# A convolution stage rebuilt: 24 frequency units in two interleaved halves of the batches, unsplit fp32 inverse transforms, filter product with exchanged partition halves

## The chip, the cores and the metric

The kernel runs on one core of one Trainium2 chip. The metric is the device time of one execution in microseconds (us); lower is better. The engines are named as the profile names them: PE (TensorE), DVE (VectorE), ACT (ScalarE), POOL (GpSimd) and SP (SyncE, which here only issues transfers).

## The reference

```python
X = np.fft.rfft(x, axis=1)                    # x: 8 batches x 3072 x 256, fp32
F = (filt_r + 1j * filt_i)[None, :, :]
x = np.fft.irfft(X * F, n=3072, axis=1)       # the convolution; then 24576 tokens of 256
do = x @ w_skip > 0                           # routed part: the best of 8 experts
e = argmax(x[do] @ w_gate);  g = softmax(...)[e]
x[do] += g * (relu(x[do] @ w1[e]) @ w2[e])
h = x @ w_in                                  # 256 -> 2048, all tokens
g = (a0 + a1*h + a2*h^2 + a3*h^3) / (1 + |b0||h| + |b1|h^2 + 1e-6)
out = g @ w_out                               # 2048 -> 256
```

The change touches only the first three lines of this and the routing that is done along with them.

## The kernel before, in words

Three stages follow one another. `conv` computes the convolution and sorts the tokens by expert. `table` and `moe_phase` run the experts in 28 slots of 512 tokens. `ff` runs the last network in 48 groups. Nothing of a later stage starts before the last token is sorted.

Inside `conv` a transform of 3072 points is split as 48 x 64. It goes through memory three times:

- **A** (`step_a`, 64 steps: 4 pairs of batches x 16 slices): loads 96 partitions of `x` (48 points of each of two batches), multiplies by the constant `fwd` into 25 complex frequencies (100 rows for the two batches), evacuates by ACT and stores into the memory tensor `za`, one store for each batch.
- **B** (`step_b`, 50 units: 25 frequencies k x 2 halves c of the batches): loads 128 partitions of `za`, multiplies by `mid` twice (mm 0 gives real over imaginary part, mm 1 imaginary over real), multiplies each by a filter table on DVE (`mult`, tiles t), adds the two on POOL (`add`), multiplies by `midi`, evacuates by ACT and stores into `zv`. `tables` loads `mid`, `midi` and the filter tables for five frequencies at a time.
- **C** (`step_c`, 64 steps; `batch` after every four): loads `zv`, multiplies by `inv`, evacuates and stores the tokens into `yd`; then transposes them on PE, multiplies by the routing weights, transposes back, and for each of 16 batches of 1536 tokens counts the positions and issues 12 indirect transfers on POOL (`scatter`, `lst<-pair,di`), which write the token numbers into the list `lst`.

Every fp32 product of A, B and C is made of three products of rounded parts (`mm3`): ACT rounds the operand to a high part (`hi`, tiles sh, yh), DVE subtracts it to get a low part (`lo`, tiles sl, yl; 26 of the 50 in B are on POOL), and PE multiplies high by high, low by high and high by low.

The order of instructions is made at build time by `Plan`: every operation has an engine, a duration, a rank and the tiles that it reads and writes, and each engine takes, of what could start, the one of least rank. The rank is a step's time t plus an offset by kind (`C_RANK`). Before, t runs on from A through B to C by `C_STEP`. Each engine then runs its queue in that order. PSUM tiles are P (2 buffers) and Q (2).

B of a half needs every `za` of that half; C of a batch needs every `zv` of its half.

Of the kernel before, what the change touches and what calls it, by code (L numbers as in the profile page):

```python
# [14 lines left out]
ALU = mybir.AluOpType  # L15
# [7 lines left out]
NK1 = 25  # L23
# [43 lines left out]
ZLO_POOL = 26  # L67
C_SLACK, C_AHEAD, C_STEP = 0.2, 12.0, (1.955, 3.997, 3.209)
C_BUFS = {'ld': 9, 'sh': 4, 'sl': 3, 't1': 4, 't2': 2, 'ev': 3, 'kt': 2, 'rh': 2, 'rl': 3, 'lt': 2, 'P': 2, 'Q': 2, 'yh': 2, 'yl': 2}
C_RANK = {'a_load': -9.13, 'a_hi': -5.41, 'a_lo': 4.16, 'a_mm': -1.53, 'a_evac': 0.65, 'a_store': 2.61, 'k_load': -35.12, 'k_filt': -24.74, 'k_sign': -13.7, 'b_load': -16.35, 'b_hiz': -5.44, 'b_loz': -1.99, 'b_mm': -2.42, 'b_mult': -0.87, 'b_add': 3.77, 'b_hiy': 5.63, 'b_loy': 6.8, 'b_mmi': 7.04, 'b_evac': 6.58, 'b_store': 10.59, 'c_load': -10.78, 'c_hi': -2.7, 'c_lo': -1.61, 'c_mm': 3.14, 'c_evac': 1.03, 'c_store': -3.1, 'c_tr': 4.44, 'c_rhi': 3.82, 'c_rlo': 2.18, 'c_logit': 9.08, 'c_lt': 6.85, 'c_back': 7.94, 'c_l9': 9.04, 'r_top': 9.23, 'r_ex': 7.28, 'r_pick': 8.67, 'r_count': 11.74, 'r_gate': 16.29, 'r_place': 14.7, 'r_scatter': 16.76}  # L70
# [13 lines left out]
def _constants():  # L84
    k1 = np.arange(NK1)
    n1 = np.arange(N1)
    n2 = np.arange(N2)
    t = 2 * np.pi * ((n1[:, None] * k1[None, :]) % N1) / N1
    fwd = np.zeros((2, N1, 2, NK1, 2))
    inv = np.zeros((2, NK1, 2, 2, N1))  # L90
    wk = np.where((k1 == 0) | (k1 == N1 // 2), 1.0, 2.0) / SEQ
    for r in range(2):
        fwd[r, :, r, :, 0] = np.cos(t)
        fwd[r, :, r, :, 1] = -np.sin(t)
        inv[r, :, 0, r, :] = (np.cos(t) * wk).T
        inv[r, :, 1, r, :] = (-np.sin(t) * wk).T
    k = k1[:, None] + N1 * n2[None, :]
# [4 lines left out]
    mid = np.concatenate([re, im, re], 2)  # L102
    c, s = c.transpose(0, 2, 1), s.transpose(0, 2, 1)
    midi = np.concatenate([np.concatenate([c, s], 2), np.concatenate([-s, c], 2)], 1)
    sg = np.where((k == 0) | (k == SEQ // 2), 0.0, np.where(k > SEQ // 2, -1.0, 1.0))
    sgn = np.stack([np.concatenate([-sg[i], sg[i]]) for i in (0, 1)], 1)
# [6 lines left out]
        "fwd": _split(fwd.reshape(2 * N1, 4 * NK1)).transpose(1, 0, 2),  # L113
        "inv": _split(inv.reshape(4 * NK1, 2 * N1)).transpose(1, 0, 2),
        "mid": _split(mid).transpose(2, 1, 0, 3),
        "midi": _split(midi).transpose(2, 1, 0, 3),
# [109 lines left out]
class Net:  # L226
# [23 lines left out]
    def setup(self):  # L250
        nc, a = self.nc, self.a
        dp = self.pool(self.ctx, "dram", 1, DRAM)
        self.za = dp.tile([NK1, 2, N2, NB, D], F32, name="za")
        self.zv = dp.tile([NK1, 2, N2, NB, D], F32, name="zv")
# [42 lines left out]
    def conv(self):  # L297
# [3 lines left out]
        G = 5  # L301
# [4 lines left out]
        fwd = cp.tile([2 * N1, 2, 4 * NK1], F32R, name="fwd")  # L306
        inv = cp.tile([4 * NK1, 2, 2 * N1], F32R, name="inv")
# [8 lines left out]
        def ps(tag):  # L316
            return pp.tile(T, F32, tag=tag, name=tag, bufs=2)
# [13 lines left out]
        def consts():  # L331
            V.memset(lists["none"], 0.0)
            nc.gpsimd.dma_start(fwd, a["fwd"])

        def consts2():
            nc.gpsimd.dma_start(inv, a["inv"])
            nc.sync.dma_start(sgn, a["sgn"])
# [3 lines left out]
        p.op("POOL", 1.1, -100, consts, writes=["fwd"], lag=2.0)  # L341

        def step_a(u, s, t):
            o = {}
            ms = slice(4 * s, 4 * s + 4)
            x = a["x"][2 * u:2 * u + 2].rearrange("r (n m) d -> (r n) m d", n=N1)
            zo = za.rearrange("k i m b d -> b (k i) m d")
# [5 lines left out]
            def hi():  # L353
                o["h"] = tl("sh", F32R)[0:2 * N1]
                nc.scalar.copy(o["h"], o["x"])

            def lo():
                o["l"] = tl("sl", F32R)[0:2 * N1]
                V.tensor_tensor(out=o["l"], in0=o["x"], in1=o["h"].bitcast(F32), op=ALU.subtract)

            def mm():
                o["p"] = ps("PQ"[s % 2])[0:4 * NK1]
                for h in range(2):
                    hs = slice(2 * h, 2 * h + 2)
                    self.mm3(o["p"][:, hs], fwd[:, 0], fwd[:, 1], o["h"][:, hs], o["l"][:, hs])

            def evac():
                o["o"] = tl("ev")[0:4 * NK1]
# [6 lines left out]
            kx, kh, kl, kp, ko = [k + (n,) for n in "xhlpo"]  # L375
            p.op("SP", 1.1, t + R["a_load"], load, writes=[new(kx, "ld")], lag=2.0)
            p.op("ACT", act(1024, 1), t + R["a_hi"], hi, reads=[kx], writes=[new(kh, "sh")])
            p.op("DVE", dve(1024), t + R["a_lo"], lo, reads=[kx, kh], writes=[new(kl, "sl")])
            p.op("PE", 1.3, t + R["a_mm"], mm, reads=["fwd", kh, kl], writes=[new(kp, "PQ"[s % 2])])
            p.op("ACT", act(1024), t + R["a_evac"], evac, reads=[kp], writes=[new(ko, "ev")])  # L380
            for r in range(2):
                p.tile(("za", u, s, r), ("za", u, s, r), 1)
                p.op("SP", 0.57, t + R["a_store"], store, r, reads=[ko], writes=[("za", u, s, r)], lag=2.0)

        def tables(g, t):
            o = {}
            ks = slice(G * g, G * g + G)

            def load():
                kt[g] = mid, midi, fr, fi = [  # L390
                    sp.tile(s, dt, tag=n, name=n, bufs=bufs["kt"])
                    for n, s, dt in (("mid", [128, G, 2, 192], F32R), ("midi", [128, G, 2, 128], F32R), ("fr", [128, G, D], F32), ("fi", [128, G, D], F32))
                ]
                nc.gpsimd.dma_start(mid, a["mid"][:, ks])
                nc.gpsimd.dma_start(midi, a["midi"][:, ks])

            def filt(h):
                _, _, fr, fi = kt[g]
# [11 lines left out]
            new(("k", g), "mid", "kt")  # L410
            new(("f", g), "fil", "kt")
            p.op("POOL", 2.1, t + R["k_load"], load, writes=[("k", g)], lag=5.0)
            for h in range(2):
                p.op("SP", 2.0, t + R["k_filt"], filt, h, reads=[("k", g)], writes=[("f", g)], lag=2.0)
            p.op("DVE", 0.9, t + R["k_sign"], sign, reads=["inv"], writes=[("f", g)])

        def step_b(k, c, t):
            o = {}
            g, j = divmod(k, G)
            zi = za.rearrange("k i m (c b) d -> k c (i m) b d", c=2)  # L420
            zo = zv.rearrange("k i m (c b) d -> k c (i m) b d", c=2)
# [12 lines left out]

            def mm(w):
                m = kt[g][0]
                o[w] = ps("P")
                ws = slice(64 * w, 64 * w + 128)
                for h in range(2):
                    hs = slice(2 * h, 2 * h + 2)  # L440
                    self.mm3(o[w][:, hs], m[:, j, 0, ws], m[:, j, 1, ws], o["h"][:, hs], o["l"][:, hs])
# [9 lines left out]
            def mmi():  # L451
                m = kt[g][1]
                o["p"] = ps("Q")
                for h in range(2):
                    hs = slice(2 * h, 2 * h + 2)
                    self.mm3(o["p"][:, hs], m[:, j, 0], m[:, j, 1], o["h"][:, hs], o["l"][:, hs])
# [5 lines left out]
            def store():  # L462
                nc.sync.dma_start(zo[k, c], o["o"])

            q = ("b", k, c)
            K = {n: q + (n,) for n in ("z", "h", "l", 0, 1, "y0", "y1", "yh", "yl", "p", "o")}
            deps = [("za", u, s, r) for u in (2 * c, 2 * c + 1) for s in range(16) for r in range(2)]
# [653 lines left out]
```

## Time and profile before

| | |
|---|---|
| time, median of 3 runs (lowest, highest) | 3947.9 us (3943.36, 3948.54) |
| span of the profiled execution, first to last instruction | 3942.5 us |
| `conv`, to the start of the last scatter | 812.7 us |
| first expert matmul | 834.06 us |

The profiled execution has no time of its own in the profile beside its span. Against the lowest run 0.9 us lies around the span, against the median 5.4 us. All times below are from the span's start. [...]

### The profile page before, as it was taken

To read this page: it belongs to the slowest core of one execution; us is meant where nothing else is said; L and a number is where in the kernel's file an instruction comes from. 1 tells how busy PE (TensorE), PEld (TensorE's weight loads), DVE (VectorE), ACT (ScalarE), POOL (GpSimd) and SP (SyncE) were. 2 spreads that over 40 slices of the span, in tenths; PEclk is the share of its full clock that TensorE was granted. 3 is DMA by queue.
4 is the path that set the end of the run, shared out by engine and by line. 5 is a ranking of instruction groups with operands and counts; after the bars stand their busy time and mean duration, and the time that the engine had idled before them with its cause. 6 is when DMAs were issued, how large, how long until landed. Compare 5 with 4: busy or idle time off the path is not lost.

```text
span 3942.5 us, 54305 instructions
## 1 busy us (share of the span) xinstructions
PE 3594.7 (91%) x20164; PEld 3031.8 (77%) x20164; DVE 3106.5 (79%) x3100; ACT 3017.2 (77%) x3076; POOL 3029.8 (77%) x1661
## 2 busy tenths in 40 slices
PE   6978888749999997999999999999999999999998
PEld 3446656448888886888888888888888888888887
DVE  3369977636666664888888888888888888888887
ACT  5655577524333334999999999999999999999997
POOL 0058847743333334999999999999999999999998
PEclk6589999869999998999999999999999999999999
DMA  8877667434444441000000000000000000000000
GB/s 263 255 227 249 201 221 207 130 112 141 145 142 149 135 129 42 22 22 22 22 22 22 22 22 20 20 21 20 19 22 22 22 22 22 22 22 22 22 11 17
DMA packets 189361, 320.69 MB, mean 81 GB/s; under 512 B 27712, under 2 KB 138379, under 8 KB 189094
## 3 DMA queue, kind: packets, MB, share of 16 engines
q1 hardware_dynamic: 170374, 281.25, 22.7%
q0 software_dynamic: 18720, 35.93, 3.0%
q8 instruction: 161, 2.64, 0.3%
q14 instruction: 106, 0.87, 0.1%
HBM read 199.98 MB, written 119.25 MB: 81 GB/s over the span
## 4 chain that ended last, share of the span: by engine, by line
POOL 29%; PE 18%; issue 11%; ACT 10%; DVE 7%; DMA 3%; SPq 1%; POOLq 0%; DVEq 0%; ACTq 0%
POOL w L990 14%; POOL gl L1034 6%; POOL v L987 5%; PE psh L246 3%; PE psh L248 3%; PE psh L247 3%; POOL es L1021 3%; PE psa L855 3%; PE psa L857 3%; DVE t L993 3%; PE psa L856 3%; DMA wr<-in_moe_w_dram 2%; ACT u L978 2%; ACT lq L1000 1%; DVE t L997 1%
## 5 line engine op out<-in xcount | busy, mean ns | idle before, releaser
L990 POOL TENSOR_TENSOR w<-v,ha 128x1024 f32<-128x1024 f32 x384 | 923.4, 2405 | 16.4 <-DVE psr L1011 0.4
L246 PE MATMUL psh<-xh,wih 128*128 128x512 f32 x1536 | 614.8, 400 | 63.2 <-DVE t L997 59.8
L993 DVE TENSOR_TENSOR t<-u,psh 128x1024 f32<-128x1024 f32 x384 | 467.0, 1216 | 236.5 <-ACT ha L981 132.0
L248 PE MATMUL psh<-xh,wil 128*128 128x512 f32 x1536 | 606.9, 395 | 0.0
L247 PE MATMUL psh<-xl,wih 128*128 128x512 f32 x1536 | 604.6, 394 | 1.6 <-POOL xl L961 1.6
L1034 POOL TENSOR_TENSOR gl<-g,gh 128x1024 fp32r<-128x1024 f32 x240 | 578.2, 2409 | 5.0 <-ACT gh L1031 5.0
L857 PE MATMUL psa<-woh,gl 128*128 128x256 f32 x1920 | 537.6, 280 | 47.8 <-POOL gl L1034 47.8
L855 PE MATMUL psa<-woh,gh 128*128 128x256 f32 x1920 | 537.8, 280 | 0.0
L856 PE MATMUL psa<-wol,gh 128*128 128x256 f32 x1920 | 532.6, 277 | 0.0
L1043 PE MATMUL psa<-woh,gn 128*128 128x256 f32 x2304 | 520.5, 379 | 0.0
L997 DVE SCALAR_TENSOR_TENSOR t<-t,co,psh 128x1024 f32<-128x1024 f32 x384 | 490.0, 1276 | 5.1
L1043 PEld LDWEIGHTS psa<-woh,gn 128*128 128x128 f32 x2304 | 436.8, 190 | 64.3
L1000 ACT ACTIVATE lq<-w,cb 128x1024 f32<-128x1024 f32 x384 | 442.9, 1153 | 44.4 <-POOL w L990 44.2
L978 ACT ACTIVATE u<-psh,co 128x1024 f32<-128x1024 f32 x384 | 460.9, 1200 | 13.2 <-PE psh L248 9.4
L804 POOL DMA_INDIRECT yd<-yo,lt x112 | 131.2, 1171 | 402.2 <-DVE yo L801 376.6
L1004 ACT ACTIVATE psr<-lq 128x1024 f32<-128x1024 f32 x384 | 393.5, 1025 | 58.9 <-DVE gn L1028 57.7
L987 POOL TENSOR_SCALAR v<-ha,co 128x1024 f32<-128x1024 f32 x336 | 406.7, 1210 | 11.9 <-ACT ha L981 11.9
L857 PEld LDWEIGHTS psa<-woh,gl 128*128 128x128 f32 x1920 | 361.4, 188 | 58.1 <-POOL gl L1034 58.0
L246 PEld LDWEIGHTS psh<-xh,wih 128*128 128x128 f32 x1536 | 290.1, 189 | 134.2 <-issue 77.5
L981 ACT ACTIVATE ha<-psh 128x1024 f32<-128x1024 f32 x384 | 389.5, 1014 | 2.8 <-PE psh L248 2.8
L856 PEld LDWEIGHTS psa<-wol,gh 128*128 128x128 f32 x1920 | 361.1, 188 | 8.2
L1021 POOL TENSOR_TENSOR es<-qq,rs 128x1024 f32<-128x1024 f32 x144 | 345.0, 2396 | 29.0 <-ACT qq L1018 29.0
(181 smaller groups left out, 9063.7 us busy)
## 6 DMA issues: line engine op xcount, KB each, us to landing
wr<-in_moe_w_dram SPq DMA_DIRECT2D x224, 256.0 KB
za<-ev SPq DMA_DIRECT2D x128, 200.0 KB
ld<-za SPq DMA_DIRECT2D x50, 512.0 KB
zv<-ev SPq DMA_DIRECT2D x50, 512.0 KB
ld<-zv SPq DMA_DIRECT2D x128, 200.0 KB
ld<-in_x_dram SPq DMA_DIRECT2D x64, 384.0 KB
yd<-ev SPq DMA_DIRECT2D x64, 384.0 KB
x<-yd SPq DMA_DIRECT2D x48, 512.0 KB
```

The lines of the kernel that those rows point to most:

```text
L246: mm(out, wh, xh, start=start, stop=False)
L247: mm(out, wh, xl, start=False, stop=False)
L248: mm(out, wl, xh, start=False, stop=stop)
L855: mm(out, xh, wh, start=start, stop=False)
L856: mm(out, xh, wl, start=False, stop=False)
L857: mm(out, xl, wh, start=False, stop=stop)
L978: nc.scalar.activation(out=tl(i, "u"), in_=o["h", i], func=AF.Identity, scale=a[3], bias=a[2])
L987: nc.gpsimd.tensor_scalar(out=tl(i, "v"), in0=o[i, "ha"], scalar1=b[1], scalar2=b[0], op0=ALU.mult, op1=ALU.add)
L990: nc.gpsimd.tensor_tensor(out=tl(i, "w"), in0=o.pop((i, "v")), in1=o.pop((i, "ha")), op=ALU.mult)
L993: V.tensor_tensor(out=tl(i, "t2", 3), in0=o.pop((i, "u")), in1=o["h", i], op=ALU.mult)
L1034: nc.gpsimd.tensor_tensor(out=tl(i, "gl", 2, F32R), in0=o.pop((i, "g")), in1=o[i, "gh"].bitcast(F32), op=ALU.subtract)
L1043: nc.tensor.matmul(o["a"][:, c], x[:, f, 128 * c:128 * c + 128], self.woh[i][:, f], start=i == 0 and f == 0 and c % 2 == 0, stop=i == 7 an ...
```

## The change

The 25 frequencies of the first factor become 24 units. Frequency 24 is real in its transform, and so is frequency 0; they share unit 0, whose tables hold both (`_bins` gives the filter rows). A's tile has 96 rows and needs one store, and C's needs one load.

`za` and `zv` become two tensors each, one for each half of the batches, laid out with the batch outermost. A row of A's store is then 4 KB that lie together, and a row of B's transfers is four pieces of 1 KB (before it was the other way round).

A's product, B's second product and C's product take fp32 operands directly (`native`, two matmuls of 512 columns), without `hi` and `lo`. B's first product keeps the three-part form and is done once instead of twice: for the second filter product DVE reads the upper 64 partitions of the PSUM tile and writes the lower 64, and then the other way round.

The order: A of the first half, then A of the second half among B of the first, then B of the second half among C of the first, then C of the second half, with new ranks and durations. `tables` runs for each half, four frequencies at a time. `fwd`, `inv` and `midi` go through SP's queue instead of POOL's. PSUM tiles are P (3 buffers) and a small S (2).

```diff
-NK1 = 25
+NK = 24
-ZLO_POOL = 26
-C_SLACK, C_AHEAD, C_STEP = 0.2, 12.0, (1.955, 3.997, 3.209)
+ZLO_POOL = (0, 1, 2, 6, 8, 12, 14, 16, 19, 28, 29, 35, 42, 43)
+C_SLACK, C_AHEAD = 0.188, 18.19
+C_PACE = ((1.831, None, None), (4.868, 6.169, None), (None, 8.8, 6.593), (None, None, 5.384))
+C_START = (0.0, 62.39, 71.2, 224.0, 227.63, 440.01)
...
-        self.za = dp.tile([NK1, 2, N2, NB, D], F32, name="za")
+        self.za = [dp.tile([NB // 2, NK, 2, N2, D], F32, name=f"za{c}") for c in range(2)]
...
-            return pp.tile(T, F32, tag=tag, name=tag, bufs=2)
+            return pp.tile(T if tag == "P" else [128, 512], F32, tag=tag, name=tag, bufs=bufs[tag])
...
+        def native(out, w, x):
+            for h in range(2):
+                hs = slice(2 * h, 2 * h + 2)
+                nc.tensor.matmul(out[:, hs], w, x[:, hs], start=True, stop=True)
...
             def mm():
-                o["p"] = ps("PQ"[s % 2])[0:4 * NK1]
-                for h in range(2):
-                    hs = slice(2 * h, 2 * h + 2)
-                    self.mm3(o["p"][:, hs], fwd[:, 0], fwd[:, 1], o["h"][:, hs], o["l"][:, hs])
+                o["p"] = ps("P")[0:4 * NK]
+                native(o["p"], fwd, o["x"])
...
-            def store(r):
-                nc.sync.dma_start(zo[2 * u + r][:, ms], o["o"][2 * NK1 * r:2 * NK1 * (r + 1)])
+            def store():
+                nc.sync.dma_start(zo[:, ms], o["o"])
...
-                    for n, s, dt in (("mid", [128, G, 2, 192], F32R), ("midi", [128, G, 2, 128], F32R), ("fr", [128, G, D], F32), ("fi", [128, G, D], F32))
+                    for n, s, dt in (("mid", [128, G, 2, 128], F32R), ("midi", [128, G, 128], F32), ("fr", [128, G, D], F32), ("fi", [128, G, D], F32))
...
             def mult(w):
-                o["y", w] = tl(f"t{w + 1}")
-                V.tensor_tensor(out=o["y", w], in0=o[w], in1=kt[g][2 + w][:, j].unsqueeze(1).to_broadcast(T), op=ALU.mult)
+                o["y", w] = y = tl(f"t{w + 1}")
+                f = kt[c, g][2 + w][:, j].unsqueeze(1)
+                if w == 0:
+                    V.tensor_tensor(out=y, in0=o["x"], in1=f.to_broadcast(T), op=ALU.mult)
+                    return
+                for h in range(2):
+                    ss = slice(64 - 64 * h, 128 - 64 * h)
+                    V.tensor_tensor(out=y[64 * h:64 * h + 64], in0=o["x"][ss], in1=f[ss].to_broadcast([64, 4, D]), op=ALU.mult)
...
             def mmi():
-                m = kt[g][1]
-                o["p"] = ps("Q")
-                for h in range(2):
-                    hs = slice(2 * h, 2 * h + 2)
-                    self.mm3(o["p"][:, hs], m[:, j, 0], m[:, j, 1], o["h"][:, hs], o["l"][:, hs])
+                o["p"] = ps("P")
+                native(o["p"], kt[c, g][1][:, j], o["y"])
...
+        t = C_START
+        for u in range(4):
+            run_a(u, t[0 if u < 2 else 1] + u % 2 * 16 * C_PACE[u >= 2][0])
+        for c in range(2):
+            run_b(c, t[2 + c])
+        for b in range(16):
+            pace = C_PACE[2 + b // 8][2]
+            run_c(b, t[4 + b // 8] + b % 8 * 4 * pace, pace)
```

On POOL's queue, where B ends and the sorting is done, before (L449 is `add`, L433 `lo`, L628 `scatter`):

```order
L449 TENSOR_TENSOR t_3101<-t_3101,t_3157 128x1024
L449 TENSOR_TENSOR t_3166<-t_3166,t_3183 128x1024
L628 DMA lst<-pair,di 201216x2 x192
L830 TENSOR_LOAD over
```

and the same place of the change (L467 is `add`, L446 `lo`, L626 `scatter`):

```order
L467 TENSOR_TENSOR t_3142<-t_3142,t_3162 128x1024
L626 DMA lst<-pair,di 201216x2 x3
L467 TENSOR_TENSOR t_3279<-t_3279,t_3298 128x1024
L626 DMA lst<-pair,di 201216x2 x7
L467 TENSOR_TENSOR t_3334<-t_3334,t_3339 128x1024
L626 DMA lst<-pair,di 201216x2 x2
L467 TENSOR_TENSOR t_3429<-t_3429,t_3439 128x1024
L626 DMA lst<-pair,di 201216x2 x120
L833 TENSOR_LOAD over
```

Of the 192 scatters 72 now stand among the additions of B's second half, and 120 behind the last one.

On SP's queue, where A ends and B begins, before (L351 loads x, L372 stores za, L425 loads za, L463 stores zv):

```order
L351 DMA ld<-in_x_dram 96x1024
L372 DMA za<-ev 50x4x256 x2
L425 DMA ld<-za 128x1024
L372 DMA za<-ev 50x4x256 x6
L425 DMA ld<-za 128x1024
L372 DMA za<-ev 50x4x256 x6
L425 DMA ld<-za 128x1024 x5
L463 DMA zv<-ev 128x1024
```

and of the change where B of the first half begins (L379 loads x, L390 stores za, L438 loads za, L478 stores zv; za_60 is the first half's, za_61 the second's):

```order
L390 DMA za_60<-ev 96x1024 x3
L379 DMA ld<-in_x_dram 96x1024
L390 DMA za_60<-ev 96x1024
L412 DMA midi<-in_midi_dram 128x512
L413 DMA fr<-in_filt_r_dram 128x1024
L414 DMA fi<-in_filt_i_dram 128x1024
L438 DMA ld<-za_60 128x4x256 x2
L379 DMA ld<-in_x_dram 96x1024
L438 DMA ld<-za_60 128x4x256
L390 DMA za_61<-ev 96x1024
L379 DMA ld<-in_x_dram 96x1024
```

Loads and stores of A's second half now stand between those of B's first half; a store of A is one transfer of 96 rows instead of two of 50.

## Rows read from the trace of the kernel before

**Rows 1.** The page: span, and 40 equal slices of it in busy tenths.
```profile
span 3942.5 us, 54305 instructions
...
POOL 0058847743333334999999999999999999999998
...
DMA  8877667434444441000000000000000000000000
```

**Rows 2.** Windows by stage: A, B, C; busy us of PE, PEld, DVE, ACT, POOL; PEclk, DMA share, GB/s.
```profile
0.00:225.00 225.00, 175.76 (x394) 95.53 (x395) 82.66 (x77) 130.68 (x130) 4.27 (x11) 0.58 0.85 258
225.00:515.00 290.00, 232.07 (x892) 172.75 (x890) 260.06 (x176) 148.57 (x150) 237.28 (x82) 0.94 0.67 216
515.00:775.00 260.00, 229.70 (x1555) 155.31 (x1556) 200.06 (x502) 200.79 (x273) 175.14 (x162) 0.91 0.71 200
```

**Rows 3.** Windows of 25 us: within A, within B, and B's last one.
```profile
100.00:125.00 25.00, 23.66 (x52) 12.95 (x51) 10.07 (x9) 16.54 (x17) 0.00 (x0) 0.50 0.84 274
350.00:375.00 25.00, 22.19 (x93) 16.71 (x92) 23.55 (x17) 14.51 (x15) 24.98 (x11) 1.00 0.99 310
...
475.00:500.00 25.00, 22.11 (x92) 16.70 (x93) 25.00 (x20) 12.29 (x13) 24.58 (x8) 1.00 0.26 105
```

**Rows 4.** DMA issues: count and KB of each.
```profile
za<-ev SPq DMA_DIRECT2D x128, 200.0 KB
ld<-za SPq DMA_DIRECT2D x50, 512.0 KB
...
ld<-in_x_dram SPq DMA_DIRECT2D x64, 384.0 KB
...
lst<-fill SPq DMA_DIRECT2D x12, 131.0 KB
```

**Rows 5.** Timeline of PE in A, at the lower clock: start, us.
```profile
99.87 0.63 PE L246 MATMUL Q<-sh,fwd 96*100 96x512 f32 x1
...
100.29 0.63 PE L247 MATMUL Q<-sl,fwd 96*100 96x512 f32 x1
```

**Rows 6.** Timeline of PE at the full clock: B (two rows), then `ff`'s unsplit product.
```profile
250.66 0.40 PE L247 MATMUL P<-sl,mid 128*128 128x512 f32 x1
...
250.89 0.40 PE L248 MATMUL P<-sh,mid 128*128 128x512 f32 x1
...
2001.90 3.62 PE L1043 MATMUL psa<-woh,gn 128*128 128x256 f32 x16
```

**Rows 7.** Timeline of PE in C: from a back-transpose (L546) to the second routing product after it.
```profile
567.58 0.35 PE L546 MATMUL Q<-eye,lt 18*128 18x18 f32 x3
...
569.19 0.57 PE L535 MATMUL P<-rh,w9a 128*18 128x384 f32 x2
```

**Rows 8.** Lines of DVE in B (225 to 515): busy us, mean ns, idle before.
```profile
L433 DVE TENSOR_TENSOR yl<-t,yh 128x1024 fp32r<-128x1024 f32 x49 | 97.4, 1990 | 11.4 <-ACT yh L429 11.3
L445 DVE TENSOR_TENSOR t<-P,fi 128x1024 f32<-128x1024 f32 x48 | 58.1, 1212 | 3.9 <-PE P L248 3.6
L433 DVE TENSOR_TENSOR sl<-ld,sh 128x1024 fp32r<-128x1024 f32 x22 | 40.5, 1846 | 0.0
```

**Rows 9.** Lines of POOL and DVE in A, B and C.
```profile
L449 POOL TENSOR_TENSOR t<-t,t 128x1024 f32<-128x1024 f32 x50 | 154.5, 3096 | 262.4 <-DVE t L445 259.4 <-PE Q L248 1.6
...
L359 DVE TENSOR_TENSOR sl<-ld,sh 96x1024 fp32r<-96x1024 f32 x64 | 78.1, 1220 | 131.9 <-ACT sh L355 129.8 <-PE Q L247 2.1
L503 DVE TENSOR_TENSOR sl<-ld,sh 100x1024 fp32r<-100x1024 f32 x64 | 77.2, 1222 | 11.0 <-ACT sh L499 10.7 <-DMA ld<-zv 0.3
```

**Rows 10.** Timeline of POOL: first scatter, last two scatters.
```profile
549.96 1.88 POOL L628 DMA_INDIRECT lst<-pair,di  x1 [40.95 <-DVE di L625]
...
811.42 0.98 POOL L628 DMA_INDIRECT lst<-pair,di  x1 [0.30 <-issue]
812.71 0.98 POOL L628 DMA_INDIRECT lst<-pair,di  x1 [0.30 <-issue]
```

**Rows 11.** Waits from 520 to 830: engine, line <- cause: us, times, longest.
```profile
POOL lst L628 <- issue: 53.9, 177, 0.3
```

More of the change, by code (lines that the diff above doesn't have):

```diff
@@ L101, in _constants @@
     im = np.concatenate([-s, c], 1)
[L102 to L106, printed above, removed]
+    ct, st = c.transpose(0, 2, 1), s.transpose(0, 2, 1)
+    midi = np.concatenate([np.concatenate([ct, st], 2), np.concatenate([-st, ct], 2)], 1)
+    k = _bins()[0]
+    t = 2 * np.pi * ((n2[:, None] * k[None, :64]) % SEQ) / SEQ
+    c, s = np.cos(t), np.sin(t)
+    s[:, 0] = -((-1.0) ** n2)
+    lo = np.arange(64) < 32
+    re[0] = np.concatenate([c * lo, c * ~lo])
+    im[0] = np.concatenate([-s * lo, -s * ~lo])
+    w = np.where(np.arange(64) == 0, 1.0, 2.0)
+    midi[0] = np.concatenate([re[0] * w, im[0] * w], 1).T
+    mid = np.concatenate([re, im], 2)
+    sg = np.where(n2 >= 32, -1.0, 1.0)
+    one = np.where(n2 == 0, 0.0, 1.0)
+    sgn = np.stack([np.concatenate([x, -x]) for x in (one, sg)], 1)
     p = np.arange(128)
@@ L470, in step_b @@
-            pool = (2 * k + c) * ZLO_POOL // 50 != (2 * k + c + 1) * ZLO_POOL // 50
-            p.op("POOL" if pool else "DVE", 2.31 if pool else dve(1024), t + R["b_loz"], lo, "z", "sl", nc.gpsimd if pool else V, reads=[K["z"], K["h"]], writes=[new(K["l"], "sl")])
-            for w in range(2):
-                p.op("PE", 1.3, t + R["b_mm"] + w, mm, w, reads=[("k", g), K["h"], K["l"]], writes=[new(K[w], "P")])
-            for w in range(2):
-                p.op("DVE", dve(1024), t + R["b_mult"] + w, mult, w, reads=[K[w], ("f", g)], writes=[new(K[f"y{w}"], f"t{w + 1}")])
@@ L476, in step_b @@
[L476 to L479 removed]
+            K = {n: q + (n,) for n in ("z", "h", "l", "x", "y0", "y1", "yh", "yl", "p", "o")}
@@ new lines, in step_b @@
+            deps = [("za", u, s) for u in (2 * c, 2 * c + 1) for s in range(16)]
+            p.op("SP", 1.5, t + R["b_load"], load, reads=deps, writes=[new(K["z"], "ld")], lag=2.2)
+            p.op("ACT", act(1024, 1), t + R["b_hiz"], hi, reads=[K["z"]], writes=[new(K["h"], "sh")])
+            pool = (24 * c + k) in ZLO_POOL
+            p.op("POOL" if pool else "DVE", 3.1 if pool else 1.6, t + R["b_loz"], lo, nc.gpsimd if pool else V, reads=[K["z"], K["h"]], writes=[new(K["l"], "sl")])
+            p.op("PE", 1.39, t + R["b_mm"], mm, reads=[("k", c, g), K["h"], K["l"]], writes=[new(K["x"], "P")])
@@ L557, in step_c @@
             K = {n: k + (n,) for n in ("x", "h", "l", "p", "o", "t", "rh", "rl", "q", "s", "g")}
-            if q == 0 and h == 0 or True:
-                deps = [("zv", kk, u // 2) for kk in range(NK1)]
-            p.op("SP", 1.15, t + R["c_load"], load, reads=deps, writes=[new(K["x"], "ld")], lag=2.0)
-            p.op("ACT", act(1024, 1), t + R["c_hi"], hi, reads=[K["x"]], writes=[new(K["h"], "sh")])
-            p.op("DVE", dve(1024), t + R["c_lo"], lo, reads=[K["x"], K["h"]], writes=[new(K["l"], "sl")])
@@ L569, in step_c @@
-            p.op("PE", 0.65, t + R["c_logit"], logit, reads=[K["rh"], K["rl"], "route"], writes=[new(K["q"], "P")])
-            p.op("ACT", act(384), t + R["c_lt"], lt, reads=[K["q"]], writes=[new(K["s"], "lt")])
-            p.op("PE", 0.35, t + R["c_back"], back, reads=[K["s"]], writes=[new(K["g"], "Q")])
+            deps = [("zv", kk, u // 2) for kk in range(NK)]
+            p.op("SP", 0.98, t + R["c_load"], load, reads=deps, writes=[new(K["x"], "ld")], lag=2.2)
+            p.op("PE", 1.83, t + R["c_mm"], mm, reads=["inv", K["x"]], writes=[new(K["p"], "P")])
@@ L645, in batch @@
             for j in range(12):
-                p.op("POOL", 1.05, t + R["r_scatter"] + j, scatter, j, reads=[K["di"], K["pr"], "route"])
+                p.op("POOL", 1.285, t + R["r_scatter"] + j, scatter, j, reads=[K["di"], K["pr"], "route"])
         p.tile("base", "base", 1)
         p.op("SP", 5.0, 20, self.setup_route, writes=["route", "base"], lag=3.0)
-        p.op("POOL", 2.0, 60, consts2, writes=["inv"], lag=3.0)
-        t = 0.0
-        for u in range(NP):
+        p.op("SP", 0.2, 20, consts2, writes=["inv"], lag=3.0)
```

223 lines of the change are left out of this document (102 added, 121 removed).

## The prediction

> **What bounds the kernel now.** The page comes first. It shows that from the 17th slice on POOL is busy nine tenths of the time, while the DMA share is near nothing [rows 1]: the experts and the last network, which hardly move data. The change doesn't touch that part. What it can move is where the convolution and the sorting end, because the experts start only then, and so every microsecond taken off the last scatter comes off the kernel. That scatter starts at 812.71 [rows 10].
>
> The windows by stage are read next, for what limits each [rows 2]. In A no engine is short of time except PE, which shows 176 of 225 us at a mean clock of 0.58. The DMA engines show 0.85 and 258 GB/s. A moves 384 + 2 x 200 KB a step [rows 4], 51 MB in all. I call A bound by transfers, with PE at its lower level close behind. In B DVE has 260 of 290 us. In C POOL shows only 175 of 260 us, which misleads: beside each scatter lies 0.3 us that the waits call issue, 177 times [rows 11], and two scatters start 1.28 us apart [rows 10]. So 192 of them are a chain of at least 247 us; from 549.96 to 812.71 they took 263, so little else was late there.
>
> Two more things are to be seen. Before the first scatter POOL waits 40.95 us [rows 10], because the first batch has to come through load, product, transpose and routing. And in B's last 25 us the DMA share is down to 0.26 [rows 3], since one stage drains before the next fills.
>
> **The change part by part.** *Transfers.* A step of A is 384 KB in and 384 KB out (96 rows of 4 KB), of C the same. A unit of B is 512 KB each way, as before [rows 4]. The tables of four frequencies are, by the shapes in the diff, 512 (`mid`), 256 (`midi`) and twice 512 KB, 1792 KB, twelve times. Up to the end of C's first half that is 64 x 768 + 48 x 1024 + 32 x 768 + 12 x 1792 KB, with 2 MB for the routing's setup (twelve fills of 131 KB the largest part, rows 4) 150 MB. The bytes are about those of before. Their rate is the unknown: 258 GB/s over A's 225 us is the lower bound [rows 2], 310 GB/s at a share of 0.99 the upper one [rows 3]. I take 280, between them, since the work of other engines now stands beside every transfer, but is also queued in order with it. 150 MB at 280 GB/s are 536 us. With 5 us to the first load (estimated from the first 25 us) and 13 for the two hand-overs between halves, this part ends at 554. The 13 lies between nothing and two drains like B's last window, which each lost 0.74 x 25 = 18 us; the other half's work now covers part of them.
>
> [...] A's windows reach a share of 0.84 at 274 GB/s and don't get above it while transfers are what is waited for; B's reach 0.99 [rows 3]. [...]
>
> *TensorE.* Two products at the full clock start 0.23 us apart, at the lower level 0.42 [rows 5, 6]. The unsplit form was measured in `ff`: 16 pieces of 256 columns in 3.62 us, 0.226 each, two pieces to a matmul [rows 6]. A step's two matmuls of 512 columns then take 8 x 0.226 = 1.81 us, against 6 x 0.23 = 1.38 for the split form. So A and C each get 0.43 us a step dearer, and a unit of B falls from 18 x 0.23 = 4.14 to 1.38 + 1.81 = 3.19. C's other products (a back-transpose, the routing product, a transpose) take 1.61 from the first of the rows to the second [rows 7]. A's second half beside B's first needs 32 x 1.81 + 24 x 3.19 = 134 us, and B's second beside C's first 24 x 3.19 + 32 x 3.42 = 186. Both lie inside the transfers' time at the full clock. For A's first half alone PE needs 58 us at the full clock and about 109 at the lower, against 31 MB (its own 25.2, two groups of tables, the setup) at 280 GB/s, 111 us. So either clock is hidden there, and this stretch ends near 116.
>
> *DVE and ACT.* The low parts of A and C go, 78 and 77 us of DVE [rows 9], and with them 128 casts on ACT. In A they cost nothing now. In C they lay beside the scatters. In B `yl` goes (1.99 us), and the second product becomes two of 64 partitions. An operation on 96 partitions takes 1.22 us and one on 128 takes 1.21 [rows 8, 9], so I price each half at 1.21: 2.42 us. A unit is then 3.63, plus 34 of 48 times 1.85 for `sl`: 4.94, where before it was 2.42 + 1.99 + 0.89 (`sl` on DVE in 24 of 50) = 5.30. DVE gains little per unit; the gain is that transfers of A or C go on meanwhile. 24 units with signs take about 131 us; half of C's own work is (200 - 77)/2 = 62 [rows 2, 9]. 193 us in the busier stretch stay under the 214 that 60 MB take there at 280.
>
> *POOL.* Of 192 scatters 72 stand among the additions of B's second half. That stretch holds 24 x 3.1 + 5 x 3.1 + 72 x 1.28 = 182 us of POOL, again under 214. A scatter at the head of the queue that waits for its batch holds the additions behind it, and their units' inverses; I count nothing for it, with a rival for the other case. Behind the last addition stand 120 scatters. 24 belong to batches already sorted (31 us), and they cover the wait for the first batch of the second half, which was 41 us. So the tail is 41 + 96 x 1.284 = 164 us.
>
> **The sum.** Last addition at about 553, last scatter at 717 instead of 813: 96 us less. The tables, experts and `ff` that follow have the same instructions. 3942.5 - 96 = 3846.5 for the span; the median of the runs lies 5.4 above the profile's span, which gives 3852 us.
>
> **The rivals.**
>
> Transfers stay at A's rate of 258 GB/s, because two streams interfere as they did in A: 150/258 = 581 us, 599 with start and hand-overs, 763 with the tail, 50 us gained, 3898. For it: no window longer than 25 us comes near 310 GB/s. Against: B had no need of more, and DVE held it.
>
> Transfers go at 310: 484 us, 502 with the same 18, 666 with the tail, 147 gained, 3801. For it: the share of 0.99. Against: four resources then stand within a tenth of each other in the third stretch (60 MB take 193, DVE 193, PE 186, POOL 182), and queues in order don't fill that.
>
> POOL's head waits: each of the eight batches of C's first half finds its scatter at the head some 10 us early (a quarter of the 41 seen), and the additions behind it stall B. 80 us, 16 gained, 3932. For it: the wait existed. Against: the planner put the batches behind C's steps.
>
> On the other side: TensorE is held at its lower level through the overlapped stretches, as it was in A, where PE showed 23.7 of 25 us busy at 0.50 [rows 3] with short gaps for its operands. Then a step of A takes 3.4 us, a unit of B 2.57 + 3.41 and C's step 6.6: 253 us for the second stretch and 356 for the third, 609 where the forecast has 438 (116 to 554), 171 more, 4023. It decides where these two stretches take 96 more, 534 us, that is where the mean granted clock falls under (134 + 186)/534 = 0.60. [...] Against it here: B's clock was 0.94 and C's 0.91 with a PE no busier [rows 2].
>
> The change does nothing: it would have to leave the last scatter where it is, for example because scatters alone set it. They don't: their chain can start as soon as half of the batches are through.
>
> **How the numbers follow.** The forecast (gain of 70 to 125) gets 0.52; transfers at A's rate 0.20; transfers at the upper rate 0.13; POOL's head 0.08; the lower clock 0.05; nothing 0.02. A measurement tells 0.2% (8 us) from no change. All but the last two and a little of POOL's case are faster: 0.92, same 0.03, slower 0.05. The range goes from the fast rival to just beyond the slow transfers, 3800 to 3905. It leaves out the last three cases and some of the fast one, 2 in 10. The likeliest case alone lies between 3823 and 3878.
>
> **What would show it.** Right: the last scatter near 717; 120 scatters 1.28 us apart behind the last addition, which lies near 553; a share of the DMA engines above 0.85 from 10 to 550; unsplit products 0.23 us apart in pieces of 256 columns; half products on DVE at 1.21 us each. The price is wrong if a half product takes 0.6 us or an addition 2.4. The prediction is wrong if PE's windows from 116 to 554 show the clock under 0.60, if POOL waits for `di` among the additions, or if the DMA share stays low with all engines waiting for each other.

## The result, and the profile after

The changed kernel takes 3791.18 us (median of 4 runs, 3788.71 to 3792.91), the kernel before 3947.1 us in the same group of runs: a ratio of 0.9604, with a 95% interval of 0.9591 to 0.9618. That is 156 us faster; 96 were forecast, and the time lies under the range's low end of 3800. The profiled execution's span is 3791.1 us and its run took 3792.91: 1.8 us lie around the span, where the forecast added 5.4.

The page of the changed kernel, with the span and the lines of POOL and the DMA engines over 40 equal slices (94.8 us each), against [rows 1]:

```profile
span 3791.1 us, 52108 instructions
...
POOL 0546767333333339999999999999999999999998
...
DMA  9999974444444310000000000000000000000000
GB/s 317 341 343 286 260 194 113 151 148 144 136 146 145 126 38 20 15 23 23 23 23 23 23 23 23 23 19 16 23 23 23 23 23 23 23 23 23 18 6 17
```

POOL's long row of nines begins in the 16th slice instead of the 17th [rows 1], and the DMA engines show 9 in each of the first five slices, where they had 8, 8, 7, 7 and 6. The stages of the changed kernel need other borders than those of before, because halves overlap: the first stretch has A's first half alone, the second A's second half with B's first, the third B's second with C's first, the fourth C's second half. Windows of the changed kernel (columns as in [rows 2]; PEclk is the granted share of TensorE's full clock); the two of 25 us come first:

```profile
50.00:75.00 25.00, 20.97 (x40) 7.35 (x40) 0.00 (x0) 10.08 (x10) 0.00 (x0) 0.82 1.02 376
179.00:204.00 25.00, 20.50 (x57) 10.14 (x58) 15.92 (x13) 11.87 (x12) 16.50 (x7) 1.00 1.10 376
...
0.00:104.00 104.00, 71.71 (x136) 24.09 (x136) 2.79 (x12) 36.08 (x36) 2.08 (x7) 0.85 0.96 317
104.00:283.00 179.00, 144.49 (x372) 68.06 (x372) 123.51 (x98) 80.38 (x81) 91.55 (x39) 0.93 1.04 344
283.00:493.00 210.00, 193.71 (x906) 105.37 (x907) 194.06 (x290) 112.10 (x143) 152.16 (x105) 0.97 0.92 260
493.00:660.00 167.00, 125.91 (x765) 69.31 (x762) 73.94 (x250) 76.13 (x110) 117.45 (x120) 0.87 0.65 159
```

Two things are to be seen. The first two stretches move 317 and 344 GB/s, up to 376 in a window of 25 us, where the fullest window shown of the kernel before has 310 [rows 3]. And in the third, at 260 GB/s, PE and DVE are each busy 194 of 210 us.

The waits agree (who waits <- for what: us in all, times, longest). From 0 to 104 A's evacuation waits for earlier stores and its product for loads; from 283 to 493 little time goes to waits for transfers:

```profile
ACT ev L387 <- DMA za<-ev: 44.7, 24, 14.2
...
PE P L369 <- DMA ld<-in_x_dram: 28.4, 12, 13.3
```

```profile
ACT sh L442 <- DMA ld<-za: 7.4, 4, 5.6
...
PE P L369 <- DMA ld<-zv: 2.5, 1, 2.5
```

The timeline of POOL, at the last addition of B and at the end of the scatters, against [rows 10]:

```profile
490.30 2.38 POOL L467 TENSOR_TENSOR t<-t,t 128x1024 f32<-128x1024 f32 x1
493.27 0.99 POOL L626 DMA_INDIRECT lst<-pair,di  x1 [0.58 <-DVE l L555]
...
658.27 0.98 POOL L626 DMA_INDIRECT lst<-pair,di  x1 [0.30 <-issue]
659.56 0.98 POOL L626 DMA_INDIRECT lst<-pair,di  x1 [0.30 <-issue]
```

The last scatter starts at 659.56 instead of 812.71, 153.15 us earlier; the first expert matmul starts at 680.86 instead of 834.06, 153.20 earlier. So the gain lies in the convolution: from the last scatter to the end of the span it is 3131.5 us now and was 3129.8.

The groups of instructions up to 700 us and, from 320 to 660, POOL's waits:

```profile
L467 POOL TENSOR_TENSOR t<-t,t 128x1024 f32<-128x1024 f32 x48 | 124.7, 2599 | 101.2 <-DVE t L463 100.9
L463 DVE TENSOR_TENSOR t<-P,fi 64x1024 f32<-64x1024 f32 x96 | 117.3, 1222 | 1.5
...
L446 DVE TENSOR_TENSOR sl<-ld,sh 128x1024 fp32r<-128x1024 f32 x34 | 54.0, 1593 | 10.9 <-ACT sh L442 10.5
```

```profile
POOL lst L626 <- issue: 48.7, 165, 0.3
POOL t L467 <- DVE t L463: 15.9, 5, 6.6
POOL lst L626 <- DVE pair L614: 10.0, 5, 3.9
POOL lst L626 <- DVE di L623: 9.7, 2, 8.8
```

### The profile page after: what moved, and what is told of

Its sections match the earlier page's. It is cut to its first block, busy times and chain, and to the rows that moved or that the text cites. A ratio compares the mean times of both kernels' runs of the same rounds, so it can differ in the third digit from the quotient of the medians.

```text
span 3791.1 us, 52108 instructions
## 1 busy us (share of the span) xinstructions
PE 3490.7 (92%) x19488; PEld 2873.4 (76%) x19488; DVE 2956.6 (78%) x2984; ACT 2842.3 (75%) x2894; POOL 2950.1 (78%) x1647
## 4 chain that ended last, share of the span: by engine, by line
POOL 31%; PE 18%; ACT 12%; issue 12%; DVE 7%; DMA 2%; SPq 0%; POOLq 0%; DVEq 0%; ACTq 0%
POOL w L993 15%; POOL gl L1037 6%; POOL v L990 6%; PE psh L269 3%; PE psh L270 3%; PE psh L271 3%; PE psa L858 3%; PE psa L860 3%; PE psa L859 3%; POOL es L1024 3%; DVE t L996 3%; ACT u L981 2%; ACT lq L1003 2%; ACT ha L984 2%; ACT qq L1021 2%
```

## The experiments

Four theories of the higher rate were tried. **S**: the rows of a transfer make the rate: with A's stores and C's loads of 50 rows the DMA engines' share stays at 0.85 (A before), with 96 rows it is 0.96 (A's first half above). **O**: the second stream of work beside the first makes the rate. **W**: A was held by its chain of cast, subtraction and three-part product, which the unsplit form removes. **L**: the new layout of `za` and `zv` (rows of 4 KB instead of pieces of 1 KB) is cheaper to move.

The experiments ran where C's second half is slower than in the runs above: it takes 233 us instead of 167 in a copy of the changed kernel, and the kernel before took 4000.6 to 4014.0 us in these groups. Two of the copy's waits from 498 to 731:

```profile
POOL lst L626 <- DVE di L623: 57.7, 4, 19.7
...
DVE rl L531 <- issue: 15.4, 4, 5.4
```

In the run above the first holds 8.8 us, and DVE there has no wait of the second kind, in which the profile shows nothing that was waited for. TensorE is granted less as well, 0.75 against 0.87, while it is busy only 155 of the 233 us; what holds the engines up isn't settled. So ratios to the kernel before of the same group are compared, and the lengths of the first three stretches, which the copy repeats at 104, 184 and 210 us.

**Other cuts of the transfers.** The kernel before, with each 50-row transfer cut into 48 and 2 rows (A's stores shown; C's loads alike):

```diff
-nc.sync.dma_start(zo[2 * u + r][:, ms], o["o"][2 * NK1 * r:2 * NK1 * (r + 1)])
+for a0, a1 in ((0, 48), (48, 50)):
+    nc.sync.dma_start(zo[2 * u + r][a0:a1, ms], o["o"][2 * NK1 * r + a0:2 * NK1 * r + a1])
```

> The kernel before, with each transfer of 50 rows in A (stores of za) and C (loads of zv) issued as one of 48 rows and one of 2. Bytes, order and engine work are unchanged. Theory S (the spread: transfers of 50 rows used only a part of the DMA engines and so held A at 258 GB/s): A's first 230 us shorten by 30 to 50 us, its rate goes above 300 GB/s at a share near 1.0, the kernel falls to about 3905. Theory O (the second stream that stands beside every transfer makes the rate) and theory W (A was held by its casts, subtractions and products, which the unsplit form removed): A stays within 8 us of its time, the kernel within 10 of 3947; two more issues a step on SP could cost a few us.

Measured: 3997.35 us, ratio 0.9968 [0.9957, 0.998]. A's last store starts at 213.5 instead of 226.1, and A's share rises from 0.85 to 0.95. So S has the right direction, but the time falls by 0.3%, much less than S expected: with twice as many transfers A's rate rises only to 277 GB/s, A gets 13 us shorter and the kernel 15.

The changed kernel, with its 96-row stores and loads cut into 50, 40 and 6 rows; the control has 48, 32 and 16:

```diff
-nc.sync.dma_start(zo[:, ms], o["o"])
+for a0, a1 in ((0, 50), (50, 90), (90, 96)):
+    nc.sync.dma_start(zo[a0:a1, ms], o["o"][a0:a1])
```

> The changed kernel with each transfer of 96 rows in A (stores) and C (loads) issued as 50, 40 and 6 rows. [...] Theory S: the first 104 us (A alone, 317 GB/s) become 120 to 130, the next stretch 10 to 20 longer, the kernel 3810 to 3830. [...]

> Control to the one above: three pieces as well, of 48, 32 and 16 rows, each a multiple of 16. What it loses against the changed kernel is the price of two more issues for each transfer. All theories: within 8 us of 3791. If it is as slow as the 50, 40 and 6 rows, the number of transfers counts and not their spread.

Measured: 3931.07 us, 0.98 [0.9778, 0.9821], and 3911.52, 0.974 [0.9723, 0.9756]. The window from 50 to 100 us, where A runs alone, of the first and of the control:

```profile
50.00:100.00 50.00, 32.43 (x52) 10.22 (x53) 0.88 (x2) 13.11 (x13) 0.00 (x0) 0.73 0.81 265
```

```profile
50.00:100.00 50.00, 36.70 (x64) 11.71 (x64) 0.88 (x2) 15.89 (x16) 0.00 (x0) 0.80 0.95 292
```

The same bytes in the same number of transfers have a share of 0.81 in the one and 0.95 in the other, and A's last store starts 19 us earlier in the control (293.9 against 313.3). But three issues for one cost as well, more than the 8 us expected of the control: uncut, this window shows 371 GB/s (below). A cleaner test was needed.

**No overlap.** The changed kernel with A's second half right behind its first, and the other stages behind each other:

```diff
-C_PACE = ((1.831, None, None), (4.868, 6.169, None), (None, 8.8, 6.593), (None, None, 5.384))
-C_START = (0.0, 62.39, 71.2, 224.0, 227.63, 440.01)
+C_PACE = ((1.831, None, None), (1.831, 6.169, None), (None, 6.169, 5.384), (None, None, 5.384))
+C_START = (0.0, 62.39, 130.0, 282.0, 450.0, 625.0)
```

> The changed kernel with start times and paces that run A of both halves, then B of both, then C of both, and nothing beside another stage. All else is as in the change. Theory O: A's rate falls back towards 260 GB/s and the kernel to 3880 or more. Theory S: A alone keeps 310 GB/s or more (the 104 us for a half become about 190 for both), and only the overlap of scatters and of B's DVE work is lost: B 48 units at DVE's 4.7 us are 225 us, C again a chain of 192 scatters, 247 us and 41 before it, so the last scatter near 190 + 225 + 41 + 247 = 703 and the kernel near 3835. Theory W says the same as S here.

Measured: 3992.98 us, 0.995 [0.9934, 0.9967]. Its windows, three of 25 us within A and then A, B and C:

```profile
75.00:100.00 25.00, 22.34 (x45) 7.01 (x44) 0.00 (x0) 11.53 (x12) 0.00 (x0) 0.93 1.02 368
100.00:125.00 25.00, 24.15 (x53) 7.50 (x52) 0.00 (x0) 12.51 (x13) 0.00 (x0) 1.00 1.03 411
125.00:150.00 25.00, 19.65 (x38) 6.53 (x37) 0.88 (x2) 10.08 (x10) 0.00 (x0) 0.86 1.02 377
...
0.00:168.00 168.00, 134.76 (x269) 45.60 (x270) 7.49 (x15) 67.65 (x67) 9.12 (x10) 0.90 0.99 345
168.00:448.00 280.00, 198.10 (x473) 96.85 (x474) 260.20 (x187) 93.93 (x94) 164.38 (x69) 0.84 0.76 243
448.00:857.00 409.00, 301.66 (x1437) 159.02 (x1435) 134.41 (x448) 145.94 (x208) 187.84 (x192) 0.74 0.45 122
```

A alone reaches 411 GB/s with nothing beside it: O falls as the cause of the rate. The kernel's time alone would fit O, which put it at 3880 or more, where S put it near 3835. But what S missed lies elsewhere: B takes 280 us where 225 were expected (DVE has 260 of them), and C 409 for 288, with the same two kinds of waits as in the copy's last stretch. So the distance to the copy, 0.995 - 0.9655 = 0.0295 of 4000 us or 118 us, is what the overlap is worth in these groups; with the faster last stretch of the first runs it may be less.

**The copy, and one difference of step A at a time.**

> The changed kernel as it is, for its ratio on the chip of this group: 0.960 again under every theory, within 0.3%. It is what the other three kernels of the group are held against.

Measured: 3862.8 us, 0.9655 [0.9635, 0.9675]. It is 0.5% off 0.9604, where 0.3% was expected. C's second half, the last row here, takes 66 us more than in the run above, while the kernel before is 53 us slower:

```profile
50.00:100.00 50.00, 37.77 (x72) 12.70 (x72) 0.88 (x2) 20.14 (x20) 0.00 (x0) 0.84 1.00 371
104.00:288.00 184.00, 148.56 (x372) 69.93 (x372) 123.38 (x99) 80.67 (x81) 93.03 (x40) 0.91 1.01 334
288.00:498.00 210.00, 194.29 (x891) 104.02 (x891) 190.58 (x286) 109.95 (x141) 150.03 (x105) 0.96 0.93 258
498.00:731.00 233.00, 155.14 (x779) 82.10 (x778) 75.46 (x254) 77.51 (x112) 118.44 (x121) 0.75 0.45 115
```

The old layout per half (A's stores and C's loads twice as many, of 48 rows; B contiguous):

```diff
-self.za = [dp.tile([NB // 2, NK, 2, N2, D], F32, name=f"za{c}") for c in range(2)]
+self.za = [dp.tile([NK, 2, N2, NB // 2, D], F32, name=f"za{c}") for c in range(2)]
...
-nc.sync.dma_start(zo[:, ms], o["o"])
+for r in range(2):
+    nc.sync.dma_start(zo[2 * (u % 2) + r][:, ms], o["o"][48 * r:48 * r + 48])
```

> The changed kernel with the two intermediates laid out as before (the batch index inside the row index: A stores and C loads pieces of 1 KB, B reads and writes one contiguous block). Theory L (the new layout gives the higher rate of the first two stretches): the stretch in which A's first half runs alone falls from 317 towards the 258 GB/s of the kernel before, and the stretch after it from 344 towards 280; first half of A plus the second stretch then last about 283 x 310/265 = 330 us, so +45 us or so against the changed kernel. Theories S (the cut of the transfers) and W (the chain of cast, subtraction and three-part product): no more than the dearer small packets cost, about 52 against 47 ns per KB in A and C, -5 to +20 us.

Measured: 3873.89 us, 0.9682 [0.9661, 0.9703], 11 us over the copy. The kernel with 50-row stores put back on top of it (two rows of padding to each):

```diff
-    nc.sync.dma_start(zo[2 * (u % 2) + r][:, ms], o["o"][48 * r:48 * r + 48])
+    nc.sync.dma_start(zo[2 * (u % 2) + r][2 - 2 * r:52 - 2 * r, ms], o["o"][46 * r:46 * r + 50])
```

> The kernel a_old_layout with one thing more put back: A's stores write 50 rows each again (48 of the units, 2 of padding), as many stores as in a_old_layout. The kernel differs from a_old_layout in nothing else, so that it prices the 50-row transfer without an issue more. Theory S (a 50-row store uses part of the DMA engines): the first stretch, 109 us at 304 GB/s in a_old_layout, goes to about 118 us and 280 GB/s, the second grows by 5 to 10 us; +15 to +20 us against a_old_layout. Rival: only the 4% more bytes of the stores count, +2 us.

Measured: 3907.08 us, 0.973 [0.9713, 0.9746], 0.0048 of 4000 or 19 us over the old layout. Windows of the old layout, and then of the 50-row stores: 50 to 100 us, and each kernel's first and second stretch:

```profile
50.00:100.00 50.00, 36.28 (x68) 11.52 (x68) 0.88 (x2) 19.13 (x19) 0.00 (x0) 0.86 1.02 333
...
0.00:109.00 109.00, 70.96 (x136) 22.29 (x136) 2.79 (x12) 36.56 (x36) 2.16 (x8) 0.87 0.98 304
109.00:301.00 192.00, 152.32 (x372) 71.33 (x372) 122.97 (x99) 79.64 (x80) 92.98 (x40) 0.90 0.96 320
```

```profile
50.00:100.00 50.00, 28.86 (x52) 8.91 (x52) 0.88 (x2) 13.06 (x13) 0.00 (x0) 0.81 0.85 265
...
0.00:119.00 119.00, 71.56 (x134) 22.25 (x135) 2.04 (x11) 34.52 (x34) 2.09 (x7) 0.87 0.84 263
119.00:322.00 203.00, 151.34 (x370) 70.01 (x369) 120.48 (x96) 80.32 (x82) 90.45 (x39) 0.90 0.92 307
```

Between these two kernels stands nothing but 50 rows for 48 in as many stores (and the 4% more bytes of the stores). The share falls from 0.98 to 0.84 and the rate from 304 to 263 GB/s, that is to A's 0.85 and 258 before [rows 2]; the first two stretches grow by 10 and 11 us. By the first load of `zv`, which comes at the end of the second, it is 27 us (323.1 for 296.0). S is shown, by the size and by the lower share; which engines stood idle the profile doesn't show. L is real and small: the old layout with its doubled stores has 333 GB/s for the copy's 371 in the early window, but costs only 5 and 8 us in the first two stretches.

The three-part product in A and C, alone (A's edit; C's is alike):

```diff
-native(o["p"], fwd, o["x"])
+split3(o["p"], fwd, o)
...
+p.op("ACT", act(1024, 1), t + R["a_mm"] - 3, hi96, o, reads=[kx], writes=[new(kh, "sh")])
+p.op("DVE", 1.3, t + R["a_mm"] - 1.5, lo96, o, reads=[kx, kh], writes=[new(kl, "sl")])
```

> The changed kernel with A's and C's product in three parts again (high part cast on ScalarE, low part subtracted on VectorE). Theory W (A was held by that chain): the first stretch lasts well over 104 us, its rate falls to about 260 GB/s, and the second stretch is longer too; together +45 us and more, and with VectorE in the third stretch (194 of 210 us busy, plus 32 subtractions of 1.3 us) another +25 us: +70 us in all. Theories S and L: the first two stretches keep 317 and 344 GB/s, and only VectorE's third stretch grows: +15 to +35 us.

Measured: 3960.14 us, 0.9896 [0.9871, 0.9922], 97 us over the copy. Its first three stretches:

```profile
0.00:110.00 110.00, 71.85 (x212) 41.99 (x213) 46.43 (x48) 71.14 (x73) 3.42 (x10) 0.80 0.98 312
110.00:332.00 222.00, 163.09 (x425) 91.24 (x425) 190.91 (x126) 106.16 (x108) 96.74 (x39) 0.80 0.88 271
332.00:586.00 254.00, 199.06 (x901) 117.25 (x902) 225.72 (x301) 133.11 (x165) 160.74 (x104) 0.87 0.79 210
```

Both theories miss. With A alone the chain costs next to nothing (312 GB/s at 0.98), so W is wrong there. Where A and C stand beside B, DVE gets 67 us more in the second stretch and 35 in the third, is busy 191 of 222 and 226 of 254 us, and the stretches grow by 38 and 44. And all three differences of A together (the same edit for A alone, on top of the 50-row stores):

> The kernel a_store50 with A's product in three parts again: all three differences of step A are put back (layout, 50-row stores, cast and subtraction), and its two halves still run as in the changed kernel. If these three are the whole cause of the higher rate, the first stretch runs at the 258 GB/s of the kernel before, some 128 us for the same bytes, and the second, with VectorE's subtractions in it, takes over 215 us; +70 us against the changed kernel of the group before. If the cause lies elsewhere (in a stretch that any kernel would run at 300 GB/s so early), the first stretch stays under 118 us.

Measured: 3944.68 us, 0.9823 [0.9807, 0.984]:

```profile
0.00:125.00 125.00, 84.37 (x198) 46.15 (x198) 42.02 (x44) 66.02 (x66) 2.63 (x8) 0.62 0.83 251
125.00:370.00 245.00, 176.47 (x444) 97.66 (x445) 201.83 (x135) 113.80 (x115) 103.85 (x41) 0.76 0.86 269
```

A runs at 251 GB/s and a share of 0.83 with a PE clock of 0.62, close to A of the kernel before (258, 0.85, 0.58). Nothing of A's rate is left for a fourth difference.

**Other parts of the change.** All 96 scatters of the first half behind the last addition, by their place in the order (and with 10 buffers for `di` instead of 2):

```diff
-p.op("POOL", 1.285, t + R["r_scatter"] + j, scatter, j, reads=[K["di"], K["pr"], "route"])
+p.op("POOL", 1.285, max(t, 440.0 + b) + R["r_scatter"] + j, scatter, j, reads=[K["di"], K["pr"], "route"])
```

> The changed kernel with all 96 scatters of the first half of the batches put behind the last filter unit. If the gain from scattering the first half early is as forecast (scatters are serial on POOL at 1.284 us), 192 scatters follow the last addition instead of some 120: 192 x 1.284 = 247 us against the tail of 166 us, +80 us; the first three stretches keep their lengths. Rival: POOL's early scatters lengthen the third stretch by as much as they save behind it, so that taking them out shortens it; then within +30 us.

Measured: 3986.32 us, 0.9967 [0.9955, 0.9978], 123.5 us over the copy. The first three stretches keep 104, 184 and 209 us, so the rival falls; the tail takes 350 us for 233, 117 more where 80 were expected. In it stand windows such as this:

```profile
597.00:622.00 25.00, 1.86 (x8) 1.30 (x8) 0.00 (x0) 1.01 (x1) 19.16 (x20) 0.50 0.15 32
```

There scatters follow each other 1.28 us apart, and C's second half stands nearly still, with 1.86 us of PE. Scatters alone don't do that: the run of the changed kernel shown first has a window with as many of them and a PE that is busy throughout:

```profile
593.00:618.00 25.00, 25.00 (x151) 13.95 (x150) 13.86 (x46) 15.84 (x24) 19.21 (x20) 1.00 0.71 192
```

In the tail of this experiment DVE's waits under "issue" hold 85.8 us, the longest 41.2, and ACT's under "remote" 93.3, a releaser that the profile doesn't name further. One of them:

```profile
572.35 0.80 ACT L527 CAST rh<-P 128x768 fp32r<-128x768 f32 x1 [12.83 <-remote]
```

These are the waits of the copy's last stretch, only longer. Their cause isn't settled, and so neither are the 37 us beyond the forecast; the granted clock over the tail is lower too, 0.64 for 0.75.

The filter product as before (the first product twice, both multiplications over 128 partitions):

```diff
-p.op("PE", 1.39, t + R["b_mm"], mm, reads=[("k", c, g), K["h"], K["l"]], writes=[new(K["x"], "P")])
+for w in range(2):
+    p.op("PE", 1.39, t + R["b_mm"] + w, mm, w, reads=[("k", c, g), K["h"], K["l"]], writes=[new(K[w], "P")])
```

> The changed kernel with the filter product as before: the unit's first product is made twice (plain and exchanged), and VectorE multiplies all 128 partitions twice. VectorE saves one 64-partition product of 1.22 us a unit (-28 us in the third stretch, 194 of 210 us busy there), TensorE does six more matmuls of 0.23 us a unit at the full clock (+32 us in the third stretch, 194 busy). If TensorE decides there: third stretch 225 to 235 us, second stretch some 5 us longer, +20 to +30 us. If VectorE does: third stretch 195 to 200 us, -10 to -15 us.

Measured: 3908.82 us, 0.9735 [0.9717, 0.9754], 0.008 of 4000 or 32 us over the copy. The third stretch:

```profile
288.00:540.00 252.00, 230.46 (x1062) 134.05 (x1061) 169.36 (x268) 117.07 (x148) 152.42 (x106) 0.97 0.88 242
```

DVE has 21 us less to do than in the copy, PE 36 more, and the last addition comes 40 us later (537.2 for 497.0). The wider `mid` also brings more to move, 61 MB in this stretch for the copy's 54, but all waits for transfers in it come to 13 us. So in this kernel TensorE decides, busy 230 of 252 us. Taking DVE alone down instead, with five more subtractions on POOL:

```diff
-ZLO_POOL = (0, 1, 2, 6, 8, 12, 14, 16, 19, 28, 29, 35, 42, 43)
+ZLO_POOL = (0, 1, 2, 6, 8, 12, 14, 16, 19, 26, 28, 29, 31, 33, 35, 38, 40, 42, 43)
```

> The changed kernel with five more of the second half's subtractions on POOL instead of VectorE (19 of 48 instead of 14). VectorE loses 5 x 1.7 = 8.5 us in the third stretch, POOL gains 5 x 2.4 = 12 us where it was busy 152 of 210. If VectorE decides the third stretch: -4 to -8 us. If the transfers or TensorE do: within 2 us. If POOL's scatters are pushed back by it: up to +10 us in the tail.

Measured: 3890.11 us, 0.9686 [0.967, 0.9702], 0.0031 of 4000 or 12 us over the copy. All three forecasts miss: the last addition is at 519.5, 22.5 us later, while DVE is busy 191 us of a third stretch of now 234. POOL shows 159 busy us there, 9 more than in the copy's 210. Its waits from 288 to 522, and the copy's from 288 to 498:

```profile
POOL t L467 <- DVE t L463: 38.4, 15, 13.1
POOL lst L626 <- issue: 18.0, 66, 0.3
POOL sl L446 <- ACT sh L442: 13.0, 3, 7.3
```

```profile
POOL t L467 <- DVE t L463: 35.5, 9, 13.2
```

The wait for DVE's products is hardly longer than in the copy; new are 9 us of work and 7 of waits for casts (6.1 in the copy). POOL runs the order of the plan, so in the 13.0 us in which subtractions wait there for their casts the scatters and additions behind them are held too. That this is the whole of the 22.5 us was not taken apart. No kernel tried here beat the changed one.

## Why the prediction was wrong

**The step that failed** is the rate, "150 MB at 280 GB/s", with 310 as its upper bound. The bytes were right: 317, 344 and 260 GB/s over 104, 179 and 210 us make 149 MB. But the first two stretches together took 283 us, where the forecast's end of the second is 554 - 214 = 340. These 57 us are the miss: the last scatter came 57.4 us before the forecast's 717.

Why 280 was too low: 258 was taken as A's rate whatever the transfers' shape, and it was the rate of 50-row stores. In the changed kernel these give 263; with 48 rows it is 304, with 96 rows in one piece of 4 KB each 317. The shape is worth some 40 of the 57 us: the first load of `zv` is issued at 283.0 in the copy, at 296.0 with the old layout and at 323.1 with 50-row stores on top of it. The other 17 are about what the forecast added for the start and the two hand-overs, 5 and 13. No run takes these away, but the trace shows no such loss: the first 25 us move 286 GB/s, and the windows of 25 us at the two borders 301 (100 to 125), 295 and 321 (250 to 300).

The forecast counted nothing for the shape. Its fast rival, at 0.13, took 310 GB/s from B's share of 0.99, and 3791 lies beyond even that rival's 3801. The row to decide it by was there: A's share was 0.84 while transfers were waited for [rows 3], and 0.85 over the stage [rows 2]. (That it didn't get above 0.84 was read too sharply: after the first 25 us A's windows lie between 0.79 and 0.86.) The two kernels that differ in the rows of a store alone have 0.84 with 50 and 0.98 with 48 over their first stretch; why 50 rows have the lower share no run shows.

The upper bound failed too. 310 GB/s at 0.99 is from a window of B in which DVE was busy 23.55 of 25 us [rows 3]: a rate that sufficed, not one that was reached. A share of 0.99 looked like a ceiling, and the changed kernel moves 376 at 1.02.

**Right, by size and cause.** What bounds the kernel: the first expert product follows the last scatter by 21.3 us before and after. The tail: 493.27 to 659.56, 166.3 us for the forecast's 164, scatters 1.28 apart. That early scatters save the tail: shown, though the 117 us without them are more than the 92 of their own chain. The half product: 1222 ns for 1.21. A's unsplit step on PE: 25 matmuls in one run of 10.89 us, four to a step, 1.74 us for 1.81. The clock: 0.93 and 0.97 in the overlapped stretches, so the slow rival's condition (under 0.60) was never near. POOL's head: the scatters' waits for `pair` and `di` hold 19.7 us in all, for a rival that wanted 80. The work in the third stretch: PE 194 us for 186, DVE 194 for 193.

**Right by size, wrong in cause.** The third stretch took 210 us for the forecast's 214, which is luck. The forecast let transfers decide it, 60 MB at 280 GB/s. It moves 55 MB at 260, well under the 344 of the stretch before, and waits little for them. What decides is the work of the engines: 36 us more of PE lengthen it by 42, and five more subtractions on POOL by 22.5. PE and DVE at 194 us each and POOL's order stand so close that no run here says which of them ends last in the changed kernel itself.

**Too dear.** POOL's addition took 2.60 us for 3.10, DVE's subtraction 1.59 for 1.85. Neither bounded a stretch alone.

**Costed at nothing, and it wasn't.** The prediction let the low parts and casts of A and C go for free, as costing nothing in A and lying beside the scatters in C. This is no part of the miss, since its 193 us of DVE leave them out, but it hides what the unsplit form is worth. In A alone it holds (312 GB/s with them). Beside B, DVE is busy 191 of 222 and 226 of 254 us with them, and the kernel takes 97 us more. Alone, A gains 6 us from the unsplit form; nearly all of its worth lies where the halves overlap.

## What to carry to other kernels

Before a stage's transfer rate is used as a bound, look at its DMA share. Here it stayed near 0.84 while transfers were waited for, and the shape of the transfers (48 or 96 rows instead of 50) moved the rate (263 GB/s to 304 and more), while the overlap wasn't needed for it. A window in which another engine is full shows what the transfers needed, not what they can do. When stages are made to overlap, sum each engine over both: work that lay hidden in either stage alone can become the bound of the two together, and in a queue that runs in order a small shift of work can cost more than its duration, as POOL's five subtractions did (9 us more of work, 22.5 us more of time).

## What was not expected of the hardware

Loads and stores together moved 411 GB/s over 25 us with A alone (share 1.03), where 310 seemed full in the kernel before. Cutting transfers has its own price: 371 GB/s fell to 292 with three issues for one at nearly the same share (1.00 and 0.95). And POOL's additions got 0.5 us shorter each without being touched, 2.60 for 3.10, beside a DVE that no longer has `yl`, 1.99 us a unit before [rows 8, 9]. With the subtractions of A and C back on DVE the 48 additions take 2.73 us each for the copy's 2.62. Whether DVE's work beside them sets their length, no run here took apart.
